# Attention and a 2-D FFT filter on one core: filter rows go from SBUF to SBUF, the last stage's pairs alternate, weight splits and flags stand apart

## The chip, the cores and the metric

The kernel runs on one core of a Trainium2 chip. A core has TensorE (PE in the profile; PEld is its loading of weights), VectorE (DVE), ScalarE (ACT), GpSimd (POOL) and SyncE (SP), and 16 DMA engines that serve the queues of SP, ACT and POOL. The metric is the time of one launch on the device in microseconds (us), as a median of several runs.

## The reference

The input x has 2048 rows of 1024 numbers in float32. Two layers follow one another, each an attention block and a spectral block, both behind a LayerNorm and both added to x:

```python
def _A_ref(x, wqkv, wo):
    qkv = (x @ wqkv).reshape(B, S, 3, H, Dh)          # H = 32 heads of 32
    ...
    scores = jnp.einsum("bhqd,bhkd->bhqk", q, k) * (Dh ** -0.5)
    p = _softmax(scores, axis=-1)
    o = jnp.einsum("bhqk,bhkd->bhqd", p, v)
    return o.transpose(0, 2, 1, 3).reshape(B, S, D) @ wo

def _B_ref(x, w_r, w_i):
    X = jnp.fft.rfft2(x, axes=(-2, -1))
    X = X * (w_r + 1j * w_i)
    return jnp.fft.irfft2(X, s=(S, D), axes=(-2, -1))

x = x + _A_ref(_layernorm(x), A_wqkv, A_wo)
x = x + _B_ref(_layernorm(x), B_w_r, B_w_i)
x = x + _A_ref(_layernorm(x), A_wqkv, A_wo)
x = x + _B_ref(_layernorm(x), B_w_r, B_w_i)
```

## The kernel before

`build` runs `attention` and then `spectral` for layer 0 and for layer 1. Much of the order is written out by hand: inside `tc.manual_schedule(engines=...)` the named engines take their instructions in the order of the code, and the other engines are ordered by the framework's scheduler. Behind both layers stands a general path that runs only if the flag `bad` is set; it isn't taken here.

**The spectral block.** The 2-D transform is done as products with constant matrices of sines and cosines. A first stage (`t1`, `fa`) turns the normalized input into 32 groups that stand in SBUF (`bh`). The middle is cut into 32 units (`UNITS`; 30 with four frequencies, the two at i = 14 and 15 with five), and a loop of 36 iterations runs over them as a pipeline. Iteration i does the forward transform along the rows for unit i (`fb`, products with `cb`, L1122, whose results ACT copies to B), splits the filtered unit i - 2 in two half-precision parts (`halves`, L1179 on ACT and L1180 on DVE), does the transform along the columns and the filter of unit i - 1 (`fc`: PE L1154, then DVE L1161 to L1164 and POOL L1168 and L1169), the first inverse step of unit i - 3 (`binv`, products with `cbi`, copied to U at L1115 by ACT) and the second of unit i - 4 (`cinv`, PE L1199 to L1202). `fc` ends with the load of the filter weights of the unit three further on (`loadw`, L1089), and in odd iterations 128 rows of the block's input y are loaded (L1235). The order of PE, ACT and SP in this loop is the order of the code.

What `cinv` leaves is a tile T of 128 partitions, four matrices j of 128 columns (256 KB). ACT copies it out of PSUM (L1204) into one of three buffers. The 128 partitions of a matrix are two halves r of 64 rows q. The next stage wants a matrix half as one partition of 64 x 128 numbers (32 KB): it sums over units, so units have to lie along the partitions. This turning of the layout goes by way of memory: SP stores T to `zt` in memory (L1205), and for every two units `turn` (L1209) reads 16 rows of 32 KB back into 16 partitions of `turned` (R or big in the rows of the trace, by layer). Which row lands on which partition is set by `row(i, r, j)` (L32), and the constant `mi` holds its rows in the same order.

**The last stage** of the block multiplies `turned` with `mi` (`ai`, L1252) in eight steps a, each in an even part (g = 0) and an odd part (g = 1, which is added to the even part in PSUM). `even(a)` needs only the rows of units 0 to 15; ACT scales its result (L1258) and POOL adds it to x (L1260). `odd(a)` needs the rows of units 16 to 31; DVE adds and subtracts its result (L1267). Four PSUM buffers hold the parts under way. The even parts 0 to 3 stand ahead of the first odd part, and behind odd(1) to odd(4) stands one more even part each. In layer 0 the splits of layer 1's first weights (`prep`) and statistics on DVE are done beside these steps, in layer 1 every step sends 1 MB of output (L1288).

**The flags.** `combine_flags` folds what was observed of the value ranges into the one flag `bad`: small operations on DVE, a transpose on PE, a reduction on DVE (L1426), a product of one number on PE (L1428), and two operations on DVE (L1430, L1431). In layer 1 it is run in three pieces, in the iterations 20, 21 and 22 of the loop.

Of the kernel before, what the change touches and what calls it, by code (L numbers as in the profile page):

```python
# [29 lines left out]


def row(i, r, j):  # L32
    return 8 * (8 * (i % 2) + 2 * j + r) + i % 16 // 2


def spec_consts():
# [303 lines left out]
PH0 = [("v", 0), ("k", 0), ("q", 0)]  # L340


def attention(nc, tc, layer, ap, xin, yd, wts, wo, cst, dram, flags):

# [295 lines left out]


    vk = [v_tiles(PH0[0], t) for t in range(8)]
    pre = [iter(()) if layer else prep(ph, m) for ph, m in zip(PH0, (lambda: load_x(1), None, lambda: load_x(4)))]

    def steps(g, n):
        for _ in range(n):
# [2 lines left out]
    with tc.manual_schedule(engines={mybir.EngineType.PE, mybir.EngineType.DVE, mybir.EngineType.Activation}):  # L651
        steps(pre[0], 1)
        for t in range(2, 4):
            load_x(t)
        for w in pre[1:]:
            steps(w, 1)
        for t in range(5, 10):
            load_x(t)
        save_x(range(8))
        m = [tile_root(nc, ap, cst, flags, layer, t) for t in range(4)]  # L660
        if layer == 0:
            for _ in range(2):
                next(m[0])
                steps(pre[0], 1)
        xn = norm_x(0, *flags.pop("rb"), 512)
        p = turn_x(xn)
        with tc.issue_after(flags["pin"].ins) if layer else nullcontext():
            next(m[1])
        steps(pre[0], 1)
        next(m[1])  # L670
        root = flags.pop("rb")
        run(pre[0])
        next(m[2])
        split_x(0, p, 4)
        xn = norm_x(1, *root)
        steps(vk[0], 8)
        next(m[2])
        root = flags.pop("rb")
        next(m[3])
        p = turn_x(xn)  # L680
        split_x(1, p, 8)
        next(m[3])
        xn = norm_x(2, *root)
        steps(vk[0], 12)
        p = turn_x(xn)
        split_x(2, p, 8)
        xn = norm_x(3, *flags.pop("rb"))
        high = flags["xn"]
        run(vk.pop(0))
        steps(vk[0], 8)  # L690
        p = turn_x(xn)
        split_x(3, p, 8)
        run(vk.pop(0))
# [307 lines left out]
    ps.close()  # L1001


def spectral(nc, tc, ap, yd, xout, a, cst, zt, fast, flags=None, nxt=None, join=None):

    ident = cst["ident"]
    psum, mid, work = Pools(tc, None), Pools(tc, "left"), Pools(tc, "left")
# [185 lines left out]
    def cinv(i):  # L1193
        g, k1, fs = UNITS[i]
        n = len(fs)
        U = Ut.pop(i)
        pt = ps.tile([128, 4, 128], F32, name="ps")
        for j in range(4 if n == 4 else 3):
            nc.tensor.matmul(pt[:, j], C["ci"][:, 8 * g + fs[j]], U[:, j], start=True, stop=True)  # L1199
        if n == 5:  # L1200
            for j in range(2):
                nc.tensor.matmul(pt[64 * j:64 * j + 64, 3], C["ci"][:, 8 * g + fs[3 + j], 0:64], U[:, 4 + j], start=True, stop=True)  # L1202
        t_ = p4.tile([128, 4, 128], F32, name="T")
        nc.scalar.copy(t_, pt)  # L1204
        nc.sync.dma_start(zt[i].rearrange("j p n -> p j n"), t_)  # L1205

    def turn(i):
        r0 = row(i, 0, 0)
        return nc.sync.dma_start(turned[r0:r0 + 121:8, UNITS[i][0]],  # L1209
                                 zt[i:i + 2].rearrange("i j (r q) n -> (i j r) q n", q=64))  # L1210

    for i in range(lead):
        loadw(i)
# [1 line left out]
    with tc.manual_schedule(engines=set(hold)) if fast else nullcontext():  # L1215
        for i in range(36):
            if i < 32:
                fb(i)
            if 0 <= i - 2 < 32 and fast:
                halves(i - 2)  # L1220
            if 0 <= i - 1 < 32:
                fc(i - 1)
            if 0 <= i - 3 < 32:
                binv(i - 3)
            if 0 <= i - 4 < 32:
                cinv(i - 4)
            if 7 <= i and i % 2:
                turn(i - 7)
            if i == 20 and join:
                joined = join(ps)  # L1230
            if 20 <= i < 23 and join:
                next(joined, None)
            if i % 2 and i < 32:
                t = i // 2
                nc.sync.dma_start(rest[:, t], yd[t * 128:(t + 1) * 128, :])  # L1235
        back = turn(30)
    psum.close()
    work.close()
    mid.close()
# [28 lines left out]
                if a == 7 and (t.start or op == ALU.subtract):  # L1268
                    next(m, None)

    with tc.manual_schedule(engines={mybir.EngineType.PE, mybir.EngineType.DVE}):
        for a in range(4):
            even(a)
        for a in range(8):
            odd(a)
            if 1 <= a < 5:
                even(a + 3)
            if nxt is not None:
                with tc.issue_after(back.ins) if a == 0 else nullcontext():
                    for _ in range(2):  # L1280
                        next(nxt, None)
                if 4 <= a < 4 + NST // 2:
                    for t in range(2 * a - 8, 2 * a - 6):
                        nc.vector.bn_stats(flags["st"][:, t, 0], ap.x[:, t, 0:512])
            else:
                sl = slice(a * 128, a * 128 + 128)
                if a < 7:
                    nc.sync.dma_start(xout[:, sl].rearrange("(t p) d -> p t d", p=128), ap.x[:, :, sl])  # L1288
                else:
                    for t, q in ((0, nc.sync), (8, nc.scalar)):  # L1290
                        q.dma_start(xout[t * 128:t * 128 + 1024, sl].rearrange("(t p) d -> p t d", p=128), ap.x[:, t:t + 8, sl])
# [112 lines left out]
def combine_flags(nc, ps, pool, flags, cst):  # L1404

    f = pool.tile([128, 6], F32, name="f4")
    fw, fb = (pool.tile([128, 1], F32, name=n) for n in ("fwm", "fwbm"))
    for m, n in ((fw, "w"), (fb, "wb")):
        nc.vector.reduce_max(m, flags[n], axis=AX.X)
    nc.vector.tensor_scalar(fw, fw, 1.0 / SW, None, op0=ALU.mult)  # L1410
    v = pool.tile([128, 1], F32, name="fv")
    nc.vector.tensor_reduce(v, flags["mv"][:, :, 1], axis=AX.X, op=ALU.min)
    nc.vector.tensor_scalar(f[:, 0:1], v, 1e-10, None, op0=ALU.is_ge)
    r = pool.tile([128, 1], F32, name="frm")
    nc.vector.reduce_max(r, flags["r"], axis=AX.X)
    nc.vector.tensor_scalar(f[:, 1:2], r, 1e20, None, op0=ALU.is_le)
    nc.vector.tensor_scalar(f[:, 2:3], fw, 1.0, None, op0=ALU.is_le)
    nc.vector.tensor_scalar(f[:, 3:4], fb, 2.0 ** -4, None, op0=ALU.is_le)
    nc.vector.tensor_scalar(f[:, 0:4], f[:, 0:4], -1.0, 1.0, op0=ALU.mult, op1=ALU.add)
    nc.vector.tensor_scalar(f[:, 4:5], fw, 2.0 ** -7, None, op0=ALU.is_ge)  # L1420
    nc.vector.tensor_scalar(f[:, 5:6], fb, 2.0 ** -12, None, op0=ALU.is_ge)
    yield
    t = ps.tile([128, 4, 128], F32, name="ps")
    nc.tensor.transpose(t[0:6, 0], f, cst["ident"])
    m = pool.tile([6, 1], F32, name="fa")
    nc.vector.reduce_max(m, t[0:6, 0], axis=AX.X)  # L1426
    yield
    nc.tensor.matmul(t[0:1, 1, 0:1], m, cst["sign"][0:6], start=True, stop=True)  # L1428
    b = pool.tile([1, 1], F32, name="fb")
    nc.vector.tensor_scalar(b, t[0:1, 1, 0:1], 2.0, 1.0, op0=ALU.add, op1=ALU.min)  # L1430
    nc.vector.tensor_copy(flags["bad"], b)  # L1431
# [6 lines left out]
def build(nc, tc, a):  # L1438
    with ExitStack() as ctx:
# [20 lines left out]
        }  # L1460
        nc.vector.memset(flags["r"], 0.0)
        x1 = dr.tile([2048, 1024], F32, name="x1")
        zt = dr.tile([32, 4, 128, 128], F32, name="zt")
        ap = AttnPools(tc)
        ap.open_small()
        x = a["x"]
        for o in (0, 512):
            nc.sync.dma_start(ap.x[:, 0, o:o + 512], x[0:128, o:o + 512])
        wts = [Weights(nc, ap, a["wp"], True, [flags["w"][:, i:i + 1] for i in range(32)], []),
               Weights(nc, ap, a["wp"], None, [], [])]  # L1470
        for layer in range(2):
            y = dr.tile([2048, 1024], F32, name=f"y{layer}")
            attention(nc, tc, layer, ap, x, y, wts[layer], a["wo"], cst, dr, flags)
            x = a["out"] if layer else x1
            if layer:
                spectral(nc, tc, ap, y, x, a, cst, zt, True, join=lambda ps: combine_flags(nc, ps, cp, flags, cst))
            else:
                spectral(nc, tc, ap, y, x, a, cst, zt, True, flags, (s for ph in PH0 for s in wts[1].prep(ph)))
        ap.close()
        bad = nc.values_load(flags["bad"][0:1, 0:1], min_val=0, max_val=1)  # L1480
        with tc.If(bad > 0):
            x = a["x"]
            for layer in range(2):
                y = dr.tile([2048, 1024], F32, name=f"gy{layer}")
                general_attention(nc, tc, x, y, a["wp"], a["wo"], cst)
                ap = AttnPools(tc)
                load_norm(nc, tc, cst, ap, y)
                x = a["out"] if layer else x1
                spectral(nc, tc, ap, y, x, a, cst, zt, False)
                ap.close()  # L1490


# [26 lines left out]
```

## Time and profile before

The launch takes 3677.62 us, the median of 3 runs (3676.18 to 3678.14). The page and the trace come from one profiled execution.

| | |
|---|---|
| Profiled execution | 3676.38 us, span 3674.6 us |
| Granted TensorE clock, mean over the span | 0.995 of full speed |
| Instructions | 80167 |
| Packets of all DMAs | 238284, 307.73 MB |
| HBM read / written | 165.65 MB / 135.20 MB |
| Stores of T (L1205) | 64, 256.0 KB each, 3.9 us from issue to landing |

The page begins with the busy time of each engine. Then it cuts the span into 40 slices of 91.9 us each. In the rows below, one digit is the busy share of a slice in tenths (9 is 90% or more), and DMA is the mean share of the 16 DMA engines:

```profile
PE   8999999999999999999899999999999999999997
...
ACT  5788888888888967768647888888888889677685
...
DMA  7122222232232442227651232323222324421378
```

The spectral blocks are the two places behind the first slice where the DMA row rises to 5 to 8 (slices 19 to 21, and 39 and 40): there the weights of the filter, y, T and the rows are moved. Between them the DMA share is 0.1 to 0.4.

### The profile page before, as it was taken

The numbers are of one execution on the slowest core, as the hardware profiler recorded it, in microseconds if no ns is written. First come the engines' busy times: TensorE is split into PE (matmuls) and PEld (weight loads), VectorE is DVE, ScalarE is ACT, GpSimd is POOL, SyncE is SP. The second block draws the span as 40 slices with busy tenths as digits, with TensorE's granted clock in tenths as the row PEclk, the third lists the DMA queues.
The fourth block names the chain that finished last, engine by engine and source line by source line (L and its number), as shares of the span: only waits on it lengthen the run. The fifth ranks groups of instructions, "written<-read, shape, count | busy, mean of one in ns | idle before, by whom it ended". The sixth has DMA issues, their size and how long they took to land. (4 is left out here: it accounts for less than half of the span.)

```text
span 3674.6 us, 80167 instructions
## 1 busy us (share of the span) xinstructions
PE 3600.5 (98%) x32663; PEld 1589.4 (43%) x32663; DVE 3104.2 (84%) x3726; ACT 2903.9 (79%) x3571; POOL 674.7 (18%) x802
## 2 busy tenths in 40 slices
PE   8999999999999999999899999999999999999997
PEld 5333433343344333378753334333433433333887
DVE  7799899989998988886568998999899989788754
ACT  5788888888888967768647888888888889677685
POOL 1022112211221110014510111111111111100144
PEclk9999999999999999999999999999999999999999
DMA  7122222232232442227651232323222324421378
GB/s 200 21 53 53 50 53 54 57 49 54 49 63 48 101 110 73 81 107 198 186 166 21 54 61 48 58 49 60 42 56 47 64 52 103 107 78 70 122 208 222
DMA packets 238284, 307.73 MB, mean 84 GB/s; under 512 B 77392, under 2 KB 156752, under 8 KB 236368
## 3 DMA queue, kind: packets, MB, share of 16 engines
q1 hardware_dynamic: 198944, 228.49, 20.6%
q0 software_dynamic: 37632, 73.43, 14.0%
q8 instruction: 258, 4.23, 0.5%
q14 instruction: 122, 1.00, 0.1%
q10 hardware_dynamic: 1328, 0.59, 0.1%
HBM read 165.65 MB, written 135.20 MB: 82 GB/s over the span
## 5 line engine op out<-in xcount | busy, mean ns | idle before, releaser
L740 ACT ACTIVATE p<-s,bias 128x1024 f32<-128x1024 f32 x2048 | 2170.8, 1112 | 457.6 <-PE s L736 439.3
L759 DVE TENSOR_TENSOR acc<-acc,p 128x1024 f32<-128x1024 f32 x896 | 1043.5, 1217 | 56.0 <-ACT p L740 55.0
L759 DVE TENSOR_TENSOR big<-big,p 128x1024 f32<-128x1024 f32 x448 | 522.2, 1218 | 38.5 <-ACT p L740 37.7
L759 DVE TENSOR_TENSOR R<-R,p 128x1024 f32<-128x1024 f32 x448 | 522.0, 1218 | 31.3 <-ACT p L740 30.1
L746 PE MATMUL o<-p,big 128*32 128x512 f32 x4096 | 492.5, 598 | 0.0
L746 PE MATMUL o<-p,R 128*32 128x512 f32 x4096 | 492.5, 598 | 0.0
L426 PEld LDWEIGHTS <-wqk 128*128 128x128 f16 x3072 | 275.6, 98 | 420.1 <-issue 127.3
L426 PE MATMUL x<-R,wqk 128*128 128x512 f16 x1440 | 338.1, 380 | 1.9 <-ACT big L488 1.2
L426 PE MATMUL x<-big,wqk 128*128 128x512 f16 x1440 | 338.2, 380 | 1.4 <-ACT R L488 0.7
L736 PEld LDWEIGHTS <-R 32*128 32x128 f16 x6144 | 114.8, 92 | 370.6 <-issue 312.8
L736 PEld LDWEIGHTS <-big 32*128 32x128 f16 x6144 | 114.2, 92 | 370.2 <-issue 312.0
L746 PEld LDWEIGHTS o<-p,big 128*32 128x32 f32 x4096 | 106.8, 109 | 261.7 <-issue 261.7
L746 PEld LDWEIGHTS o<-p,R 128*32 128x32 f32 x4096 | 106.8, 109 | 261.7 <-issue 261.7
L736 PE MATMUL s<-R 32*128 32x512 f16 x3072 | 213.7, 377 | 0.1
L736 PE MATMUL s<-Q,big 32*128 32x512 f16 x3072 | 212.7, 377 | 1.0 <-DVE mqk L460 1.0
L736 PE MATMUL s<-Q,R 32*128 32x512 f16 x3072 | 212.6, 378 | 1.0 <-DVE mqk L460 1.0
L736 PE MATMUL s<-big 32*128 32x512 f16 x3072 | 212.5, 377 | 0.1
L765 POOL DMA_DIRECT2D zd<-acc x112 | 92.4, 825 | 653.8 <-DVE z L775 304.0
L484 PE MATMUL x<-wv,big 128*128 128x256 f16 x1392 | 165.4, 275 | 3.0 <-DVE R L219 2.2
L484 PEld LDWEIGHTS <-big 128*128 128x128 f16 x1536 | 145.5, 98 | 48.9 <-issue 28.6
L484 PE MATMUL x<-wv,R 128*128 128x256 f16 x1392 | 165.4, 275 | 0.9 <-ACT R L392 0.9
L484 PEld LDWEIGHTS <-R 128*128 128x128 f16 x1536 | 145.5, 98 | 46.8 <-issue 26.1
(519 smaller groups left out, 4112.0 us busy)
## 6 DMA issues: line engine op xcount, KB each, us to landing
zd<-acc POOLq DMA_DIRECT2D x112, 256.0 KB, 4.2
wst<-in_wp SPq DMA_DIRECT2D x96, 256.0 KB, 3.3
zt<-T SPq DMA_DIRECT2D x64, 256.0 KB, 3.9
w<-in_w SPq DMA_DIRECT2D x60, 256.0 KB, 3.1
zd<-R POOLq DMA_DIRECT2D x56, 256.0 KB, 4.1
zt<-zr SPq DMA_DIRECT2D x224, 64.0 KB, 2.7
od<-ohl SPq DMA_DIRECT2D x56, 256.0 KB, 2.4
zd<-big POOLq DMA_DIRECT2D x56, 256.0 KB, 4.1
```

The lines of the kernel that those rows point to most:

```text
L426: nc.tensor.matmul(ps, a, b, start=i == 0, stop=i == 23)
L484: nc.tensor.matmul(ps[:, j], x[c][:, d, o:o + 128], w[:, n, d], start=i == 0, stop=i == 23)
L736: nc.tensor.matmul(s[h // 2][:, h % 2], K[g][r, a, kt * 128:kt * 128 + 128], Q[g][r, b, c * 512:c * 512 + 512], start=i == 0, stop=i == 2)
L740: nc.scalar.activation(p, s[hf], AF.Exp, bias=bias[g], scale=SCALE / (SQ * SQ))
L746: nc.tensor.matmul(O[g, c][32 * h:32 * h + 32], V[g][:, kt, 32 * h:32 * h + 32], P[g, c, kt, h // 2][:, h % 2], start=kt == 0, stop=kt == ...
L759: last_add = nc.vector.tensor_add(a, a, p)
L765: nc.gpsimd.dma_start(z, a[32 * j:32 * j + 32].rearrange("p a j n -> p (a j n)"), max_dma_last_dim=2048, **({"accum_op": ALU.add} if j els ...
```

## The change

Three edits are made.

**Rows.** `cinv` no longer stores T to memory. It issues four transfers, one for each matrix j, straight from T into two partitions of `turned`: r0 for the half r = 0, and r0 + 64 for r = 1. `zt` and `turn` are gone, and `row` is changed so that the two halves of a matrix lie 64 partitions apart; `mi` follows, since it is built with `row`.

**The last stage.** Two even parts stand ahead of odd(0), and behind each of odd(0) to odd(5) stands the even part two further on. ACT now also takes its instructions there in the order of the code. The splits of layer 1's weights are handed out by a table of steps, and those of the query chunk but the first step are passed on to `attention` as `rest`, which runs them ahead of its first query chunk.

**The flags.** `combine_flags` has more points at which it stops (`yield`), and is run in the iterations 12 to 23, one piece in each.

```diff
 def row(i, r, j):
-    return 8 * (8 * (i % 2) + 2 * j + r) + i % 16 // 2
+    return 64 * r + 16 * j + i % 16
...
-    pre = [iter(()) if layer else prep(ph, m) for ph, m in zip(PH0, (lambda: load_x(1), None, lambda: load_x(4)))]
+    pre = [iter(()), iter(()), rest] if layer else [prep(ph, m) for ph, m in zip(PH0, (lambda: load_x(1), None, lambda: load_x(4)))]
...
         t_ = p4.tile([128, 4, 128], F32, name="T")
         nc.scalar.copy(t_, pt)
-        nc.sync.dma_start(zt[i].rearrange("j p n -> p j n"), t_)
-
-    def turn(i):
-        r0 = row(i, 0, 0)
-        return nc.sync.dma_start(turned[r0:r0 + 121:8, UNITS[i][0]],
-                                 zt[i:i + 2].rearrange("i j (r q) n -> (i j r) q n", q=64))
+        for j in range(4):
+            r0 = row(i, 0, j)
+            back = nc.sync.dma_start(turned[r0:r0 + 65:64, g], t_[:, j])
+        return back
...
             if 0 <= i - 4 < 32:
-                cinv(i - 4)
-            if 7 <= i and i % 2:
-                turn(i - 7)
-            if i == 20 and join:
+                back = cinv(i - 4)
+            if i == 12 and join:
                 joined = join(ps)
-            if 20 <= i < 23 and join:
+            if 12 <= i < 24 and join:
                 next(joined, None)
...
-        back = turn(30)
...
-    with tc.manual_schedule(engines={mybir.EngineType.PE, mybir.EngineType.DVE}):
-        for a in range(4):
+    with tc.manual_schedule(engines={mybir.EngineType.PE, mybir.EngineType.DVE, mybir.EngineType.Activation}):
+        for a in range(2):
             even(a)
         for a in range(8):
             odd(a)
-            if 1 <= a < 5:
-                even(a + 3)
+            if a < 6:
+                even(a + 2)
             if nxt is not None:
                 with tc.issue_after(back.ins) if a == 0 else nullcontext():
-                    for _ in range(2):
+                    for _ in range((2, 1, 1, 1, 2, 1, 1, 0)[a]):
                         next(nxt, None)
...
-    for m, n in ((fw, "w"), (fb, "wb")):
-        nc.vector.reduce_max(m, flags[n], axis=AX.X)
+    nc.vector.reduce_max(fw, flags["w"], axis=AX.X)
+    yield
+    nc.vector.reduce_max(fb, flags["wb"], axis=AX.X)
+    yield
...
             else:
-                spectral(nc, tc, ap, y, x, a, cst, zt, True, flags, (s for ph in PH0 for s in wts[1].prep(ph)))
+                pre = [wts[1].prep(ph) for ph in PH0]
+                spectral(nc, tc, ap, y, x, a, cst, True, flags, chain(*pre[:2], islice(pre[2], 1)))
```

The order of the built instructions shows where this puts them. Below stands SP's queue in layer 0's loop, about the loads of the two units with five frequencies, before the change (line, operation, destination <- source with buffer numbers, shape; x4 is the same row four times):

```order
L1089 DMA w_20175<-in_w 128x640
L1205 DMA zt_85<-T_20205 128x4x128
L1089 DMA w_20242<-in_w 128x640
L1205 DMA zt_85<-T_20272 128x4x128
L1209 DMA R_93<-zt_85 16x8192
L1235 DMA big_89<-y0_133 128x1024
L1089 DMA w_20319<-in_w 128x512
L1205 DMA zt_85<-T_20345 128x4x128
L1089 DMA w_20400<-in_w 128x512
L1205 DMA zt_85<-T_20426 128x4x128
```

And the same place after it (the lines are those of the changed kernel, L1208 is the new transfer and L1232 the load of y):

```order
L1090 DMA w_20195<-in_w 128x640
L1208 DMA R_92<-T_20225 2x64x128 x4
L1090 DMA w_20265<-in_w 128x640
L1208 DMA R_92<-T_20295 2x64x128 x4
L1232 DMA big_88<-y0_132 128x1024
L1090 DMA w_20344<-in_w 128x512
L1208 DMA R_92<-T_20370 2x64x128 x4
L1090 DMA w_20428<-in_w 128x512
L1208 DMA R_92<-T_20454 2x64x128 x4
L1232 DMA big_88<-y0_132 128x1024
```

One store of T for each unit has become four transfers into R, and the return after every second unit is gone.

PE's rows at the beginning of layer 0's last stage before the change (the number in a name is the PSUM buffer's, its second appearance is the odd part):

```order
L1252 MATMUL ai_21658<-mi_66,R_93 128x128 x8
L1252 MATMUL ai_21670<-mi_66,R_93 128x128 x8
L1252 MATMUL ai_21682<-mi_66,R_93 128x128 x8
L1252 MATMUL ai_21694<-mi_66,R_93 128x128 x8
L1252 MATMUL ai_21658<-mi_66,R_93 128x128 x8
L1252 MATMUL ai_21670<-mi_66,R_93 128x128 x8
L1252 MATMUL ai_21737<-mi_66,R_93 128x128 x8
L1252 MATMUL ai_21682<-mi_66,R_93 128x128 x8
L1252 MATMUL ai_21763<-mi_66,R_93 128x128 x8
```

And after it:

```order
L1248 MATMUL ai_21737<-mi_66,R_92 128x128 x8
L1248 MATMUL ai_21749<-mi_66,R_92 128x128 x8
L1248 MATMUL ai_21737<-mi_66,R_92 128x128 x8
L1248 MATMUL ai_21771<-mi_66,R_92 128x128 x8
L1248 MATMUL ai_21749<-mi_66,R_92 128x128 x8
L1248 MATMUL ai_21804<-mi_66,R_92 128x128 x8
L1248 MATMUL ai_21771<-mi_66,R_92 128x128 x8
```

Before, the first odd part is the fifth row; now it is the third, and from there on one even part and one odd part alternate.

DVE's rows in layer 1's loop at the end of the flags before the change (`fa` is the reduction behind the transpose, `fb` and `fi` read the product of one number in the same PSUM tile; G, t_ and H belong to the units):

```order
L1164 TENSOR_TENSOR t__42405<-ps_42400,w_42195 128x256
L1180 TENSOR_TENSOR H_42333<-G_42332,H_42333 128x2x256
L1180 TENSOR_TENSOR H_42399<-G_42398,H_42399 128x2x256
L1426 TENSOR_REDUCE fa_42524<-ps_42522 6x1
L1430 TENSOR_SCALAR fb_42591<-ps_42522 1x1
L1431 CAST fi_82<-fb_42591 1x1
L1161 TENSOR_TENSOR G_42478<-ps_42480,w_42271 128x256
```

And after it:

```order
L1181 TENSOR_TENSOR H_42308<-G_42307,H_42308 128x2x256
L1428 TENSOR_REDUCE fa_42516<-ps_42514 6x1
L1181 TENSOR_TENSOR H_42388<-G_42387,H_42388 128x2x256
L1162 TENSOR_TENSOR G_42467<-ps_42469,w_42251 128x256
L1163 TENSOR_TENSOR t__42474<-ps_42469,w_42251 128x256
L1164 TENSOR_TENSOR G_42467<-ps_42469,w_42251 128x256
L1165 TENSOR_TENSOR t__42474<-ps_42469,w_42251 128x256
L1432 TENSOR_SCALAR fb_42586<-ps_42514 1x1
L1433 CAST fi_82<-fb_42586 1x1
```

The two last operations of the flags stood right behind the reduction; now five operations of the units stand between.

More of the change, by code (lines that the diff above doesn't have):

```diff
@@ L2 @@
 from contextlib import ExitStack, nullcontext
+from itertools import chain, islice
 import concourse.bass as bass
@@ L340, with attention @@
 PH0 = [("v", 0), ("k", 0), ("q", 0)]
-def attention(nc, tc, layer, ap, xin, yd, wts, wo, cst, dram, flags):
+def attention(nc, tc, layer, ap, xin, yd, wts, wo, cst, dram, flags, rest=()):
     W, prep = wts.W, wts.prep
@@ L654, in attention @@
             load_x(t)
-        for w in pre[1:]:
+        for w in pre[1:] if layer == 0 else ():
             steps(w, 1)
@@ L1001, in load_norm, with spectral @@
     ps.close()
-def spectral(nc, tc, ap, yd, xout, a, cst, zt, fast, flags=None, nxt=None, join=None):
+def spectral(nc, tc, ap, yd, xout, a, cst, fast, flags=None, nxt=None, join=None):
     ident = cst["ident"]
@@ L1412, in combine_flags @@
     nc.vector.tensor_reduce(v, flags["mv"][:, :, 1], axis=AX.X, op=ALU.min)
+    yield
     nc.vector.tensor_scalar(f[:, 0:1], v, 1e-10, None, op0=ALU.is_ge)
@@ L1415, in combine_flags @@
     nc.vector.reduce_max(r, flags["r"], axis=AX.X)
+    yield
     nc.vector.tensor_scalar(f[:, 1:2], r, 1e20, None, op0=ALU.is_le)
     nc.vector.tensor_scalar(f[:, 2:3], fw, 1.0, None, op0=ALU.is_le)
+    yield
     nc.vector.tensor_scalar(f[:, 3:4], fb, 2.0 ** -4, None, op0=ALU.is_le)
     nc.vector.tensor_scalar(f[:, 0:4], f[:, 0:4], -1.0, 1.0, op0=ALU.mult, op1=ALU.add)
+    yield
     nc.vector.tensor_scalar(f[:, 4:5], fw, 2.0 ** -7, None, op0=ALU.is_ge)
@@ L1462, in build @@
         x1 = dr.tile([2048, 1024], F32, name="x1")
-        zt = dr.tile([32, 4, 128, 128], F32, name="zt")
         ap = AttnPools(tc)
@@ L1470, in build @@
                Weights(nc, ap, a["wp"], None, [], [])]
+        pre = []
         for layer in range(2):
             y = dr.tile([2048, 1024], F32, name=f"y{layer}")
-            attention(nc, tc, layer, ap, x, y, wts[layer], a["wo"], cst, dr, flags)
+            attention(nc, tc, layer, ap, x, y, wts[layer], a["wo"], cst, dr, flags, *pre[2:])
             x = a["out"] if layer else x1
             if layer:
-                spectral(nc, tc, ap, y, x, a, cst, zt, True, join=lambda ps: combine_flags(nc, ps, cp, flags, cst))
+                spectral(nc, tc, ap, y, x, a, cst, True, join=lambda ps: combine_flags(nc, ps, cp, flags, cst))
             else:
-                spectral(nc, tc, ap, y, x, a, cst, zt, True, flags, (s for ph in PH0 for s in wts[1].prep(ph)))
+                pre = [wts[1].prep(ph) for ph in PH0]
+                spectral(nc, tc, ap, y, x, a, cst, True, flags, chain(*pre[:2], islice(pre[2], 1)))
         ap.close()
@@ L1488, in build @@
                 x = a["out"] if layer else x1
-                spectral(nc, tc, ap, y, x, a, cst, zt, False)
+                spectral(nc, tc, ap, y, x, a, cst, False)
                 ap.close()
```

## The prediction

> **What bounds the kernel now.** I read the page first, then the busy time by stretches, then the chain of waits, then the order in time on TensorE and on the DMA queues.
>
> The page's first part gives busy time, share of the span and instructions by engine:
>
> ```profile
> PE 3600.5 (98%) x32663; PEld 1589.4 (43%) x32663; DVE 3104.2 (84%) x3726; ACT 2903.9 (79%) x3571; POOL 674.7 (18%) x802
> ```
>
> TensorE (PE) is busy for 98% of the span. But the change touches only the spectral stages and their ends, so what counts is how things stand there. The busy time by stretches has for each start:end its length, then busy microseconds of PE, PEld, DVE, ACT and POOL, the granted clock, the DMA engines' mean busy share and GB/s:
>
> ```profile
> 1680.00:1720.00 40.00, 39.38 (x348) 35.30 (x346) 24.86 (x63) 34.41 (x90) 17.98 (x28) 1.00 0.77 212
> 3640.00:3675.00 35.00, 18.10 (x160) 17.94 (x160) 16.70 (x17) 4.10 (x4) 11.54 (x5) 0.80 0.89 244
> ```
>
> In the middle of a spectral loop PE works 39.38 of 40 us. The DMA engines are at 0.77, not far behind: a change of the DMA work can make them the bound. In the last 35 us they carry the end at 0.89, writing the output. The order in time on PE (start, length, matmuls, in brackets idle time before and who ended it) gives the pace of the loop and the first stop of layer 0's last stage:
>
> ```profile
> 1799.81 7.41 PE L1252 MATMUL ai<-mi,R 128*128 128x128 f32 x64 [0.72 <-ACT T L1204]
> 1809.48 3.81 PE L1252 MATMUL ai<-mi,R 128*128 128x128 f32 x32 [2.26 <-DMA wst<-in_wp]
> ...
> 3583.75 1.47 PE L1122 MATMUL ps<-cb,R 128*128 128x256 f16 x12
> ...
> 3588.16 1.47 PE L1122 MATMUL ps<-cb,R 128*128 128x256 f16 x12
> ```
>
> From one unit's first product to the next one's pass 4.41 us (3588.16 - 3583.75). At 1799.81 four even parts run, 1.85 us each (7.41 / 4); then PE has nothing until the filter rows of the last units are in SBUF, and the odd parts start at 1809.48. The releaser named is another DMA, but an odd part reads only the rows and the constant mi, so I take it to be the last row transfer. The chain that ended last shows the same place in layer 1:
>
> ```profile
> 3626.55 3.99 DMA zt<-T
> ...
> 3630.59 4.98 DMA big<-zt
> ...
> 3635.91 2.04 PE ai L1252 x16
> ```
>
> T goes to memory in 3.99 us and comes back in 4.98 us, and the odd parts start at 3635.91.
>
> **What the transfers cost now.** The queue's own rows (start, time of the issue) show where a layer's row traffic begins, and what an issue like the new one takes:
>
> ```profile
> 1660.65 0.38 SPq L1205 DMA_DIRECT2D zt<-T  x1
> ...
> 3489.40 0.38 SPq L1205 DMA_DIRECT2D zt<-T  x1
> ...
> 3590.49 0.48 SPq L1209 DMA_DIRECT2D big<-zt  x1
> ```
>
> So the row traffic now spans 148.8 us in layer 0 (1660.65 to 1809.48) and 146.5 us in layer 1 (3489.40 to 3635.91), with all of it hidden but the last stop.
>
> The DMA view of one stretch counts packets by size and gives the share of the 16 engines' time that they took. From 1662 to 1666 almost only T is being moved, in pieces of 512 bytes:
>
> ```profile
> DMA packets 559, 0.31 MB, mean 77 GB/s; under 512 B 31, under 2 KB 535, under 8 KB 559
> q1 hardware_dynamic: 559, 0.31, 25.6%
> ```
>
> From 3400 to 3410 one 512 KB store goes in 4 KB pieces:
>
> ```profile
> DMA packets 144, 0.52 MB, mean 52 GB/s; under 512 B 16, under 2 KB 16, under 8 KB 144
> q1 hardware_dynamic: 144, 0.52, 12.8%
> ```
>
> From 3631 to 3636 one return of rows goes from zt to 16 partitions:
>
> ```profile
> DMA packets 48, 0.52 MB, mean 105 GB/s; under 512 B 32, under 2 KB 32, under 8 KB 32
> q1 hardware_dynamic: 48, 0.52, 48.1%
> ```
>
> The second: 12.8% of 160 us are 20.5 us for 128 pieces, 160 ns for 4 KB. The first: 25.6% of 64 us are 16.4 us; 24 pieces of 2 KB at half of 160 ns are 1.9 us, which leaves 14.5 us for 504 pieces, **28.7 ns for 512 bytes**. The third is the one that matters most: 16 data packets (48 less 32 small ones) for a transfer with 16 destination rows. One packet is one row of 32 KB, 2.4 us each (48.1% of 80 us by 16), and 38.5 us of packets fit in 5 us, so they run side by side. **This transfer was cut by its destination rows.**
>
> **The change part by part.**
>
> *Rows from SBUF to SBUF.* Per unit the change takes away one store of T (256 KB) and half a return (512 KB), and issues four transfers of 64 KB. Each has 128 source rows and two destination rows, r0 and r0 + 64, and each destination row is filled by 64 pieces of 512 bytes, since a source partition holds only 128 numbers of it. That is 512 pieces for a unit, where T's store alone had 512 before. If the work is cut by destination rows as in the row above, two engines carry each transfer and the other fourteen nothing. If these are the same two each time, each has 4 x 64 = 256 pieces a unit: 256 x 28.7 ns = 7.35 us, against the 4.41 us that PE needs for a unit. The two engines keep up only below 12.5 ns a piece (4.41 less some 1.2 us of other loads, by 256).
>
> The loads that those two engines share with the rest are these, in the stretch 1660 to 1806:
>
> ```profile
> big<-y SPq DMA_DIRECT2D x14, 512.0 KB, 7.0
> w<-in_w SPq DMA_DIRECT2D x24, 256.0 KB, 3.6
> ...
> w<-in_w SPq DMA_DIRECT2D x2, 320.0 KB, 4.8
> ```
>
> One of 16 engines carries of a y load 8 pieces of 4 KB (1.28 us) and of a w load 8 of 2 KB (0.64 us; 0.80 for the large ones). The sum on one of the two engines, for one layer: rows 32 x 256 x 28.7 ns = 235.1 us, y 14 x 1.28 = 17.9 us, w 24 x 0.64 + 2 x 0.80 = 17.0 us, together **270.0 us**. They start with the first T as before, and the odd parts start when the last row is in: 270.0 - 148.8 = +121.2 us in layer 0 and 270.0 - 146.5 = +123.5 us in layer 1, **+244.7 us** in all.
>
> The wait that this adds: T has three buffers, so ACT's copy into T (L1204) waits for the rows of three units before. Behind it in ACT's order stand the next unit's copies of B and U (L1115), for which PE waits; PE then runs at the transfers' pace. On SP the next w load and y load stand behind four issues, 4 x 0.48 = 1.9 us instead of some 0.6, inside 4.41 us: nothing, unless the queue fills, and then the two engines are the limit anyway. POOL's queue has no part in it.
>
> No row shows a piece that goes from SBUF to SBUF. Bounds by the nearest rows: at the rate of the 4 KB pieces 160 / 8 = 20.0 ns; at that of the 32 KB packets into a single partition 2.4 us / 64 = 37.6 ns. I take 28.7 ns, of the row that already reads T in the same pieces. The ends give 163.8 + 34.9 = 198.7 us and 308.0 + 34.9 = 342.9 us a layer, so +102.1 us and +390.5 us in all.
>
> [...]
>
> *Pairs alternate.* Only two even parts stand ahead of odd(0), and the other two now come behind it: 2 x 1.85 = 3.7 us of PE that used to lie in the stop. I cost it at nothing: in layer 1 the output's DMA (0.89 in the last stretch) covers it, in layer 0 DVE's adds and statistics. Without that cover it is 3.7 us a layer. PE will come to this stage from half idleness; at the clock of 0.80 in the row above, its 26 us here would take some 6 us more. I leave that to the range.
>
> *Weight splits and flags apart.* Two weight splits of layer 1 move into the attention, before the query chunk that needs them: nothing. The flags' last step now stands a unit behind the reduction that feeds it. Before, DVE waited there for PE:
>
> ```profile
> 3570.55 0.15 DVE L1430 TENSOR_SCALAR fb<-ps 1x1 f32<-1x1 f32 x1 [4.24 <-PE ps L1428]
> ```
>
> and PE's unit took 8.84 us instead of 4.41:
>
> ```profile
> 3570.44 1.48 PE L1122 MATMUL ps<-cb,R 128*128 128x256 f16 x12
> ...
> 3579.28 1.54 PE L1122 MATMUL ps<-cb,R 128*128 128x256 f16 x12
> ```
>
> That is worth 4.4 us where PE sets the pace. Under the rows' traffic it is worth nothing.
>
> **The rivals.** *The transfers spread (faster).* If the pieces are shared out by the source's 128 rows, or successive transfers take turns on other pairs, no engine has more to do than before, and the tail shortens. The last T is copied at 3626.55; three further issues (1.44 us) and a landing like T's (3.9 us by the page) put odd(0) at 3631.9, 4.0 us earlier; in layer 0, from a copy that ends at 1799.8, at 1805.1, 4.4 us earlier. With the flags' 4.4 us: 3676.4 - 12.8 = **3663.6 us**. For it: the engines now share T's store, which has 128 rows on both sides. Against it: the only transfer here with few destination rows had just one packet for each. It decides at the count of engines: four would still carry 128 x 28.7 ns = 3.7 us of rows and 1.1 us of loads a unit, eight 1.8 and 1.1 us, below 4.41.
>
> [...]
>
> *Each piece pays twice (slower still).* If reading from SBUF and writing to it do not overlap on an engine, a piece takes 57.4 ns: 470.2 + 34.9 = 505.1 us a layer, +714.9 us, **4391 us**. For it: nothing but that no such piece has been seen. Against it: T's pieces, read from SBUF and written to memory, already do both in 28.7 ns.
>
> **How the numbers follow.** The profiled execution took 3676.4 us, 1.2 us below the median of the runs. Two engines: 3676.4 + 244.7 = **3921 us**, chance 0.80. Spread: 3664 us, chance 0.15. Pieces twice: 4391 us, chance 0.05. The range is that of the first case, 3676.4 + 102.1 = 3778 to 3676.4 + 390.5 = 4067, and leaves out the other 0.20. What a measurement of this kernel can tell from no change is about 0.2%, 7 us: the spread case clears it unless half its gain is lost, so faster 0.13, same 0.02, slower 0.85.
>
> **What would show it.** Right: PE's period in the spectral loops near 8.6 us instead of 4.41, ACT's T copy waiting for a DMA, the DMA share in the loops falling to about 0.15 to 0.2 while nothing else is busy, and the gap from the first row transfer to the first odd part near 270 us. Wrong: the period stays at 4.41 us and the new transfers land within some 4 us of issue; then the engines share them. If the period is between, the price of a piece is what I missed.

## The result, and the profile after

The changed kernel takes **3913.9 us**, the median of 4 runs (3913.35 to 3914.88), against 3677.88 us before: a ratio of 1.0642, 95% interval 1.0624 to 1.0661, 236.0 us longer. The forecast was 3921 us, the range 3778 to 4067. The profiled execution took 3914.88 us, with a span of 3913.1 us, 238.5 us longer than the span before.

The page, first the busy time, then two rows of the 40 slices (97.8 us each):

```profile
PE 3680.7 (94%) x32663; PEld 1629.1 (42%) x32663; DVE 3114.3 (80%) x3726; ACT 2898.2 (74%) x3571; POOL 670.6 (17%) x802
...
PE   8999999999999999976589999999999999999874
...
DMA  6132223322234422333251232223222344212334
```

PE runs no more products than before (32663), though they count as 80 us more of busy time, at a mean granted clock of 0.973 against 0.995. It is now less busy in slices 18 to 20 and at the end, and in the same slices the DMA share, which used to rise to 7 and 8, stays at 2 to 4. Both wait, and the busy time by stretches shows it for the loop of layer 0:

```profile
1680.00:1720.00 40.00, 28.91 (x201) 22.94 (x201) 14.11 (x33) 19.74 (x50) 9.52 (x13) 0.89 0.32 83
```

In the same stretch before, PE was busy for 39.38 us and the DMA share was 0.77. The order in time names the wait. First ACT, then SP's queue, between two units of that loop (a line of SP's queue gives the start and the time of its issues; x4 is four of them):

```profile
1706.64 0.59 ACT L1205 COPY T<-ps 128x512 f32<-128x512 f32 x1 [5.01 <-DMA R<-T]
...
1715.28 0.58 ACT L1205 COPY T<-ps 128x512 f32<-128x512 f32 x1 [4.46 <-DMA R<-T]
```

```profile
1702.78 5.97 SPq L1208 DMA_DIRECT2D R<-T  x4
1708.85 1.58 SPq L1232 DMA_DIRECT2D big<-y  x1
1710.54 0.37 SPq L1090 DMA_DIRECT2D w<-in_w  x1
1711.00 7.68 SPq L1208 DMA_DIRECT2D R<-T  x4
```

From one copy of T to the next pass 8.64 us instead of 4.41, and ACT stands for some 5 us of them until a buffer of T comes free. SP too is held: four issues take 5.97 and 7.68 us, where an issue took 0.48 us before. With rows alone under way, the DMA view of a stretch at layer 0's end reads:

```profile
DMA packets 1509, 0.76 MB, mean 38 GB/s; under 512 B 23, under 2 KB 1509, under 8 KB 1509
...
q1 hardware_dynamic: 1509, 0.76, 14.2%
```

That is 1915 to 1935 us: many transfers are queued, and they take no more than 14.2% of 16 engines, 2.3 engines' worth (two engines that are always busy are 12.5%; with two, the spans of packets overlap a little). If transfers took turns on other engines, a full queue would show more of them. The 1486 pieces here (1509 less 23 small packets) are those of 11.6 transfers, so each transfer has two small packets; the experiments come back to that. Shared by two engines, 1486 pieces in 20 us are one piece in 26.9 ns on each. In layer 1, from 3855 to 3868 us, it is one in 23.6 ns:

```profile
DMA packets 1118, 0.56 MB, mean 43 GB/s; under 512 B 18, under 2 KB 1118, under 8 KB 1118
```

The rows' time in a layer runs from the first issue of L1208 to the odd parts (behind the stop in the last stage):

```profile
L1208 SPq DMA_DIRECT2D R<-T x128: 505/1620/4566, 1661.2 to 1933.0; - x128
L1208 SPq DMA_DIRECT2D big<-T x128: 506/1374/4451, 3627.6 to 3864.9; - x128
```

```profile
1911.71 5.90 PE L1248 MATMUL ai<-mi,R 128*128 128x128 f32 x32 [4.28 <-ACT T L1205]
1941.11 27.95 PE L1248 MATMUL ai<-mi,R 128*128 128x128 f32 x224 [23.50 <-DMA R<-T]
...
3842.90 4.55 PE L1248 MATMUL ai<-mi,big 128*128 128x128 f32 x32
3871.48 27.07 PE L1248 MATMUL ai<-mi,big 128*128 128x128 f32 x224 [24.04 <-DMA big<-T]
```

1941.11 - 1661.2 = 279.9 us in layer 0 and 3871.48 - 3627.6 = 243.9 us in layer 1, against 148.8 and 146.5 us before: +131.1 and +97.4, **+228.5 us** of the 238.5. The other 10 us lie outside: 6.6 us from layer 0's odd parts to layer 1's first transfer (1686.5 us against 1679.9), 2.9 us from layer 1's odd parts to the end (41.6 against 38.7), and 0.5 us ahead of the first transfer.

### The profile page after: what moved, and what is told of

Its sections match the earlier page's. It is cut to its first block, busy times and chain, and to the rows that moved or that the text cites. A ratio compares the mean times of both kernels' runs of the same rounds, so it can differ in the third digit from the quotient of the medians.

```text
span 3913.1 us, 80433 instructions
## 1 busy us (share of the span) xinstructions
PE 3680.7 (94%) x32663; PEld 1629.1 (42%) x32663; DVE 3114.3 (80%) x3726; ACT 2898.2 (74%) x3571; POOL 670.6 (17%) x802
## 5 line engine op out<-in xcount | busy, mean ns | idle before, releaser
L1205 ACT COPY T<-ps 128x512 f32<-128x512 f32 x64 | 37.4, 585 | 235.5 <-DMA R<-T 123.1
L1181 DVE TENSOR_TENSOR H<-G,H 128x512 f16<-128x512 f32 (+1 forms) x68 | 55.4, 819 | 162.2 <-ACT H L1180 162.0
L1155 PE MATMUL ps<-cc,B 128*128 128x128 f32 x520 | 93.7, 313 | 90.7 <-ACT B L1116 90.2
```

The lines of the kernel that those rows point to most:

```text
L1155: nc.tensor.matmul(pc[:, j].rearrange("p r f -> p (r f)"), B[:, POS[n][o + j]], C["cc"][:, 8 * g + fs[o + j]], start=True, stop=True)
L1181: nc.vector.tensor_sub(lo, gs, hi)
```

## The experiments

**The rows' part undone** (the run norows). In the changed kernel, T goes to memory and comes back as before:

```diff
-    return 64 * r + 16 * j + i % 16
+    return 8 * (8 * (i % 2) + 2 * j + r) + i % 16 // 2
...
-        for j in range(4):
-            r0 = row(i, 0, j)
-            back = nc.sync.dma_start(turned[r0:r0 + 65:64, g], t_[:, j])
+        nc.sync.dma_start(zt[i].rearrange("j p n -> p j n"), t_)
...
+            if 7 <= i and i % 2:
+                back = turn(i - 7)
```

> The changed kernel with the rows sent through memory again (store of T, return of 16 rows, the old row order); pairs, weight splits and flags stay as changed. Theory (the rows alone made the time longer, since two DMA engines carry them): the loop is back at 4.41 us a unit, the flags' step of 4.4 us is gone, and the even parts behind odd(0) cost 0 to 3.7 us a layer: 3677.9 - 4.4 = 3673.5 us, up to 3681 us. Rival (the other two edits have a share in the 236 us): clearly over 3690 us.

3682.92 us, median of 11 runs; ratio to before 1.0017 (1.0008 to 1.0026). The large loss is gone, so it takes the rows' part to make it. What is left is 0.17% slower than before, not faster: a little over the bound of 3681. The flags' gain did not come, since in this kernel the scheduler put their last operations right behind one another again, and DVE waited for PE as before:

```profile
3565.12 0.14 DVE L1437 TENSOR_SCALAR fb<-ps 1x1 f32<-1x1 f32 x1 [4.24 <-PE ps L1435]
```

**The rows' part alone** (rowsonly), put into the kernel before (the diff above, reversed).

> The kernel before with the rows alone changed (four transfers from T to two partitions each); the last stage, the splits and the flags as before. Theory (two engines carry the rows): as long as the changed kernel, 3914 us, less at most the 3.7 us a layer of even parts that lie in the stop here, so 3906 to 3920 us. Rival (the edits lengthen the time only together): well under 3900 us.

3909.35 us, ratio 1.0634 (1.0618 to 1.0651). The rows make the loss by themselves, but for some 4 us. The rows' time is that of the changed kernel, 279.6 us in layer 0 (1659.3 to 1938.89) and 244.4 in layer 1 (3621.3 to 3865.71).

**Two buffers for T** (tbufs2) in place of three.

```diff
-    pw, p4 = work("sp_pw", lead), work("sp_p4", 3)
+    pw, p4 = work("sp_pw", lead), work("sp_p4", 2)
```

> The changed kernel with two buffers for T in place of three. Theory (the two engines are always busy with rows): with two buffers one unit's rows are still under way while the next T is copied, so the time stays at 3914 us, at most 20 us more. Rival (each unit waits for the latency of its transfers, and three buffers set how many are in flight): the period goes from about 8 to about 12 us a unit, some 250 us more, about 4160 us.

3908.09 us (one run), and the rows' time is 280.4 and 241.9 us, about as with three buffers. Fewer buffers cost nothing: the wait is for something that is always busy, not for a latency that more buffers would hide.

**The suspected cost doubled** (double): each transfer is issued twice.

```diff
-        for j in range(4):
-            r0 = row(i, 0, j)
-            back = nc.sync.dma_start(turned[r0:r0 + 65:64, g], t_[:, j])
+        for j in range(8):
+            r0 = row(i, 0, j % 4)
+            back = nc.sync.dma_start(turned[r0:r0 + 65:64, g], t_[:, j % 4])
```

> The changed kernel with each of the four transfers issued twice (the same data to the same place): the suspected cost doubled. Theory (two engines carry all pieces one after the other): 2 x 32 x 256 more pieces on each engine at 23 to 28.7 ns are 377 to 470 us more, 4290 to 4385 us. Rival (the wait is the latency of a unit's transfers, or SP's issues): four more issues of 0.5 us a unit, at most 2 x 32 x 2 us = 130 us more, under 4050 us.

4330.43 us (one run), 416.5 us more than the changed kernel and inside what the engines' load gave. The first issue of each layer, and the first odd parts:

```profile
L1208 SPq DMA_DIRECT2D R<-T x256: 510/1602/4484, 1662.1 to 2157.3; - x128
L1208 SPq DMA_DIRECT2D big<-T x256: 506/1387/4542, 3852.3 to 4281.9; - x128
```

```profile
2165.49 9.78 PE L1248 MATMUL ai<-mi,R 128*128 128x128 f32 x59 [50.78 <-DMA R<-T]
...
4288.31 11.96 PE L1248 MATMUL ai<-mi,big 128*128 128x128 f32 x92 [53.44 <-issue]
```

The rows' time is now 503.4 and 436.0 us, 223.5 and 192.1 us more than with single transfers. The 32 x 256 = 8192 added pieces on an engine thus cost **27.3 ns each in layer 0 and 23.5 ns in layer 1**. That is the pace at which the rows ran alone in the changed kernel, 26.9 and 23.6 ns. What does not double is 279.9 - 223.5 = 56.4 us and 243.9 - 192.1 = 51.8 us.

**Half of the transfers from ACT's queue** (actq).

```diff
-            back = nc.sync.dma_start(turned[r0:r0 + 65:64, g], t_[:, j])
+            back = (nc.sync if j < 2 else nc.scalar).dma_start(turned[r0:r0 + 65:64, g], t_[:, j])
```

> The changed kernel with two of a unit's four transfers issued by ACT in place of SP. [...] Rival (each queue has two engines of its own): half the load on each, 128 pieces and the loads, 4.3 to 4.8 us a unit, and ACT pays its issues: 3690 to 3730 us.

Against that rival, the same engines on both queues had been put at 3895 to 3930 us. 3894.43 us (one run) is half a microsecond below these bounds: 20 us less than the changed kernel, where other engines for the second queue would have given 200 less. From 1915 to 1921 us, with rows alone under way from both queues (q1 is SP's, q10 is ACT's), the DMA view reads:

```profile
q1 hardware_dynamic: 226, 0.11, 7.7%
q10 hardware_dynamic: 226, 0.11, 7.5%
```

Together they take 15.2% of 16 engines, where one queue took 14.2%. Two queues get no more than one, so both are served by the same engines. Of the 20 us, 14.7 lie in the rows' time (274.1 and 235.0 us); what shortened it was not tried.

**One destination row for each transfer** (onerow): eight of 32 KB, the same pieces and the same layout.

```diff
         for j in range(4):
-            r0 = row(i, 0, j)
-            back = nc.sync.dma_start(turned[r0:r0 + 65:64, g], t_[:, j])
+            for r in range(2):
+                r0 = row(i, r, j)
+                back = nc.sync.dma_start(turned[r0:r0 + 1, g], t_[64 * r:64 * r + 64, j])
```

> The changed kernel with each transfer cut in two: eight transfers of 32 KB a unit, each from 64 partitions into one partition, the same 512 pieces of 512 bytes a unit and the same row order. Theory as the prediction put it (a transfer is cut by its destination rows): one row means one engine, 512 pieces on it at 23 to 28 ns are 12 to 14 us a unit, about 8 x 32 x 2 us = 500 us over the kernel before, about 4200 us. [...] Rival (SBUF to SBUF is slow however it is shared): still about 3914 us. [...]

3796.25 us, ratio 1.0328 (1.0313 to 1.0342): half of the loss is gone. That rules out the theory in its plain form (one row, one engine) and the rival (as slow however it is shared). A third time had been put down for the case that many engines share such a transfer and SP's issues, at 0.5 us each, set the pace: 4.4 to 4.7 us a unit, 3664 to 3682 us. It is not that either, and SP's queue in the loop shows one reason:

```profile
1701.34 5.79 SPq L1209 DMA_DIRECT2D R<-T  x8
1707.40 0.35 SPq L1090 DMA_DIRECT2D w<-in_w  x1
1707.85 5.76 SPq L1209 DMA_DIRECT2D R<-T  x8
1713.71 0.53 SPq L1233 DMA_DIRECT2D big<-y  x1
1714.35 0.36 SPq L1090 DMA_DIRECT2D w<-in_w  x1
1714.81 6.09 SPq L1209 DMA_DIRECT2D R<-T  x8
```

SP issues almost without a gap, eight transfers in 5.8 us (0.72 us each, where I had put 0.5), 6.4 us a unit with the loads (256 issues in the 202.7 us from 1661.9 to 1864.6). The transfers themselves land 3.7 us after their issue in the median, 2.6 us at best:

```profile
DMA to landing us min/median/max: 2.6/3.7/8.8
```

Sixty-four pieces on one engine would need 64 x 23.5 = 1.5 us for one transfer and 12 us for a unit, longer than the 6.4 us in which a unit passes here, so more than one engine carries these transfers. How many is seen in the small packets, from 1660 to 1860 us:

```profile
DMA packets 25927, 23.23 MB, mean 116 GB/s; under 512 B 4661, under 2 KB 20661, under 8 KB 25907
```

In this stretch SP issues 251 transfers of rows and 40 loads. If each load has 16 small packets, 4661 - 640 = 4021 are left, 16 for each transfer of one row. With two rows there were two. In the kernel before, the stores of T, the returns and the loads also come out at about 16 (1394 small packets for 88 transfers, from 1660 to 1806 us). My estimate from these counts is that 16 engines carry a transfer with one row and two a transfer with two: it takes each small packet for one engine, as the two small packets and the 14.2% of the full queue go together with two rows, and was not tested by itself. A further rival, that a partition of the destination can't take its pieces faster, falls too: in this run, from 1709.78 to 1710.05 us, 62 of the 64 pieces of one transfer start on their way into one partition, 4.4 ns a piece.

**Half of these issues from POOL** (onerowpool).

```diff
-                back = nc.sync.dma_start(turned[r0:r0 + 1, g], t_[64 * r:64 * r + 64, j])
+                back = (nc.gpsimd if r else nc.sync).dma_start(turned[r0:r0 + 1, g], t_[64 * r:64 * r + 64, j])
```

> onerow with the four transfers of the half r = 1 issued by POOL in place of SP. In onerow SP issues one after the other (eight in 5.8 us) and a unit takes about 6.5 us. Theory (onerow is bound by SP's issues, not by engines): SP needs 4 x 0.72 + 0.36 + 0.27 = 3.5 us a unit, POOL its 2 us of work and 4 x 0.8 us (its stores of zd), 5.2 us, so 1.2 us a unit less: 3796 - 77 = 3720 us, 3695 to 3745. Rival (32 KB transfers are slow on the engines): 3780 us or more.

3770.92 us (one run): 25 us less, a third of what was expected, and by neither theory. SP now has gaps, so it no longer sets the pace alone, but POOL's issues stand among its own work, and in one unit ACT waits for that:

```profile
1712.35 0.62 ACT L1180 CAST H<-G 128x512 f16<-128x512 f32 x1 [4.44 <-POOL G L1170]
```

What bounds this kernel was not followed further.

**The two large buffers in SBUF exchanged** (swap), since the rows' time was 36 us longer in layer 0 than in layer 1 for the same transfers:

```diff
-        self.lay(self.low("at_x", 1).tile([128, 16384], F32, name="big"),
-                 self.right("at_r", 1).tile([128, 16384], F32, name="R"))
+        self.lay(self.right("at_r", 1).tile([128, 16384], F32, name="big"),
+                 self.low("at_x", 1).tile([128, 16384], F32, name="R"))
```

> The changed kernel with the two large SBUF buffers exchanged: what lay in the one (the rows' destination in layer 0) now lies in the other. In the changed kernel a layer's rows took 279.9 us in layer 0 and 243.9 us in layer 1, from the first issue to the first odd part. Theory (the place of the destination in SBUF sets a piece's price): the two times change places, about 244 us in layer 0 and 280 us in layer 1. Rival (something else of the layer does it: what is loaded beside the rows, or the order): they stay where they are, 280 and 244 us. The total stays within 10 us of 3914 us by both.

3914.89 us (one run). The first issues and the odd parts of its two layers:

```profile
L1208 SPq DMA_DIRECT2D R<-T x128: 505/1374/4447, 1660.9 to 1897.5; - x128
L1208 SPq DMA_DIRECT2D big<-T x128: 506/1622/4898, 3591.4 to 3865.1; - x128
```

```profile
1904.51 7.75 PE L1248 MATMUL ai<-mi,R 128*128 128x128 f32 x47 [20.21 <-DMA wst<-in_wp]
...
3872.61 9.64 PE L1248 MATMUL ai<-mi,big 128*128 128x128 f32 x58 [28.75 <-DMA big<-T]
```

243.6 us in layer 0 and 281.2 us in layer 1: they have changed places. Which of the two large buffers the rows go to sets the price, and not the loads of y beside them, which go to the other buffer: with rows alone under way it is one piece in 23.6 ns in layer 0 (1270 pieces from 1880 to 1895 us) and in 27.0 ns in layer 1 (1482 from 3845 to 3865).

**The even parts** (evens4): norows with four even parts ahead of odd(0), and ACT not bound to the order of the code:

```diff
-    with tc.manual_schedule(engines={mybir.EngineType.PE, mybir.EngineType.DVE, mybir.EngineType.Activation}):
-        for a in range(2):
+    with tc.manual_schedule(engines={mybir.EngineType.PE, mybir.EngineType.DVE}):
+        for a in range(4):
...
-            if a < 6:
-                even(a + 2)
+            if 1 <= a < 5:
+                even(a + 3)
```

> The kernel norows with the last stage in the order of before (four even parts ahead of odd(0), ACT not in the order of the code there); its splits and flags stay as changed. Theory (in norows the even parts moved behind odd(0) cost 3.2 us in layer 0 and 1.9 us in layer 1, read from its trace against that of before): 5 us less than norows, so within 0.1% of the kernel before, about 3677 us. Rival (the splits handed out in other steps, or the moved flags, cost it): as long as norows, 3683 us.

3677.96 us, median of 11; ratio to before 1.0003 (0.9993 to 1.0012), against 1.0017 (1.0008 to 1.0026) with the pairs alternating. By the ratios the difference is the 5 us that were expected, but the intervals overlap, and the profiled executions of the two (3681.91 and 3680.84 us) are only 1.1 us apart. The price of this edit is thus suggested and not shown. The run undoes two things at once, the order of the parts and that of ACT.

**The flags, two tries** (flagsonly and flags2), both on the kernel before. First other iterations for the three pieces:

```diff
-            if i == 20 and join:
+            if i == 18 and join:
                 joined = join(ps)
-            if 20 <= i < 23 and join:
+            if i in (18, 20, 22) and join:
                 next(joined, None)
```

> The kernel before with the flags' three pieces run in the iterations 18, 20 and 22 in place of 20, 21 and 22, so that the two last operations on DVE stand a unit behind the reduction. (In norows the scheduler had put them right behind the reduction again, and the unit of 8.8 us was there as before.) Theory: the wait of 4.2 us on DVE and PE's long unit go, 4.4 us less, a ratio of 0.9988. Rival (a PSUM buffer held for two iterations more stops PE elsewhere): no change, 1.0000, or slower.

3679.82 us, ratio 1.0007 (0.9998 to 1.0016): no gain, as the rival had it, but not by its mechanism. DVE stops at each of the flags' operations:

```profile
3561.71 0.28 DVE L1426 TENSOR_REDUCE fa<-ps 6x1 f32<-6x128 f32 x1 [4.70 <-PE ps L1424]
3561.92 0.40 DVE L1161 TENSOR_TENSOR G<-ps,w 128x256 f32<-128x256 f32 x1
...
3573.54 0.15 DVE L1430 TENSOR_SCALAR fb<-ps 1x1 f32<-1x1 f32 x1 [3.07 <-PE ps L1428]
3573.72 0.14 DVE L1431 CAST fi<-fb 1x1 int32<-1x1 f32 x1
3573.79 0.40 DVE L1161 TENSOR_TENSOR G<-ps,w 128x256 f32<-128x256 f32 x1
```

The products of a unit (L1161) come right behind and are late each time. So the second try leaves the iterations at 20, 21 and 22, ties the flags' second and third piece behind a unit's products, and changes nothing else:

```diff
-                fc(i - 1)
+                last = fc(i - 1)
...
-                next(joined, None)
+                with tc.issue_after(last.ins) if i > 20 else nullcontext():
+                    next(joined, None)
```

> The kernel before with the flags' second and third piece tied on DVE behind the products of the unit in whose iteration they stand (L1161 to L1164), as the changed kernel has its last piece; PE's order is as before. In flagsonly the two waits of DVE for PE (4.7 and 3.1 us) stood ahead of a unit's products, and the units took 7.3 and 8.3 us. Theory (DVE's place decides, not the distance between the flags' operations): no product waits behind a flag, PE keeps its 4.41 us a unit, 4 us less than before, a ratio of 0.9988 to 0.999. Rival (the lost time isn't on the path that sets the end of the loop): 1.0000.

3673.95 us, median of 11; ratio 0.9989 (0.9980 to 0.9998). PE's first products of the units around the flags, in order of time:

```profile
3568.23 1.47 PE L1122 MATMUL ps<-cb,R 128*128 128x256 f16 x12
...
3572.85 1.48 PE L1122 MATMUL ps<-cb,R 128*128 128x256 f16 x12
...
3577.27 1.47 PE L1122 MATMUL ps<-cb,R 128*128 128x256 f16 x12
```

4.62 and 4.42 us: the unit of 8.84 us is gone. This is the one version that is faster than the kernel before, by 0.1%, with the upper end of its interval just below 1.

**The last two units alone from SBUF to SBUF** (tail), on top of flagsonly, with one row a transfer:

```diff
-        nc.sync.dma_start(zt[i].rearrange("j p n -> p j n"), t_)
+        if i < 30:
+            nc.sync.dma_start(zt[i].rearrange("j p n -> p j n"), t_)
+            return
+        for j in range(4):
+            for r in range(2):
+                r0 = row(i, r, j)
+                back = (nc.scalar if r and i == 31 else nc.sync).dma_start(turned[r0:r0 + 1, g], t_[64 * r:64 * r + 64, j])
```

> flagsonly with the rows of the last two units alone (30 and 31) sent from SBUF to SBUF, in eight transfers of one destination row each, those of unit 31 half from SP and half from ACT; the other thirty units go through memory. Theory (16 engines share such a transfer, and what it costs is the issue, some 0.7 us): unit 31's rows are issued within 3 us and land 3.7 us later, about 3 us a layer earlier than by memory: 6 us less than flagsonly, a ratio to before of 0.997. Rival (unit 30's eight issues stand ahead on SP, and the landing takes as long as store and return): no gain on flagsonly.

3694.68 us, ratio 1.0049 (1.0035 to 1.0062): slower than before. In SP's queue the return of units 28 and 29 now stands behind twelve issues:

```profile
1797.75 0.55 SPq L1216 DMA_DIRECT2D R<-zt  x1
1800.17 10.71 SPq L1211 DMA_DIRECT2D R<-T  x12
1810.93 0.59 SPq L1216 DMA_DIRECT2D R<-zt  x1
```

With 4.98 us, as such a return took before, it lands at 1815.9, and the odd parts of layer 0 started at 1816.74 instead of 1809.48. Counted from the first even part, the odd parts start 5.8 us later than before in layer 0 and 4.8 us later in layer 1; where the rest of the 17 us lies was not followed. The edit put the return there; whether a tail with the return ahead would gain was not tried.

## Why the prediction was right

*Two engines carry the rows: right.* The runs norows and rowsonly give the whole loss to this edit, tbufs2 and double show a load and not a latency, actq shows that the engines are the same from another queue, and the full queue at 14.2% of 16 engines, with two small packets for each transfer, shows their number. The word that the prediction gave to the cause was too narrow: it said that a transfer is cut by its destination rows. onerow, with one row a transfer, is not confined to one engine: it leaves 16 small packets for the 64 pieces of a transfer, where two rows leave two, and a unit passes in 6.4 us where one engine would need 12. What decides how many engines share a transfer was not shown beyond these two cases.

*The sum: right by terms that missed on both sides.* It said 270.0 us a layer: 235.1 for the pieces and 34.9 for the other loads.

| us | predicted | layer 0 | layer 1 |
|---|---|---|---|
| price of a piece, ns | 28.7 | 27.3 | 23.5 |
| 8192 pieces on one engine | 235.1 | 223.5 | 192.1 |
| all else in the rows' time | 34.9 | 56.4 | 51.8 |
| rows' time | 270.0 | 279.9 | 243.9 |
| more than before | 121.2 / 123.5 | 131.1 | 97.4 |

The price came from T's pieces on their way to memory and was too high, by 1.4 and 5.2 ns. A part of that can be read from the views: the prediction divided the time of packets by their number, and on a busy engine packets overlap. In the changed kernel, the 14.2% from 1915 to 1935 us are 45.4 us of packets, some 30 ns a piece, while a piece passed every 26.9 ns. Against that, the rest was mis-sized: beside the pieces 16.9 and 21.5 us a layer more pass than the packets of w and y take by themselves. The runs don't divide it. That the total came within 7 us of the forecast is in part luck, since the errors went against each other: the rows' time was 9.9 us longer than forecast in layer 0 and 26.1 us shorter in layer 1, and 10 us lie outside it.

*The rest of the sum: not at nothing.* 10 us lie outside the rows' time, and the sum had none there. In rowsonly, whose span is 232.6 us longer than before, 3.9 us lie outside it, so some 6 come with the other two edits, within a scatter of a few us (in kernels with the same code up to there, layer 0's first transfer starts anywhere from 1658.7 to 1662.1 us). norows and evens4 suggest some 5 us for the last stage's edit, which the prediction cost at nothing, or at 7.4 us if nothing covered it. Their traces show less of it: from the first even part to PE's next stage in layer 0, and to the end in layer 1, pass 44.1 and 51.0 us in norows and 43.3 and 50.2 in evens4, so 0.8 us a layer. So whether the cover that the prediction named (DVE in layer 0, the output in layer 1) holds in full stays open. The clock that it left to the range cost little: the 224 products from odd(0) on took 27.95 and 27.07 us, where norows took 26.88 and 26.87.

*The flags: right in size.* What they are worth under the rows' traffic was not measured by itself. Where PE sets the pace, flags2 shows 0.11% (4 us; 0.7 to 7.4 by the interval), against 4.4 us predicted. But what frees them is DVE's place behind the unit's products, not the distance that the change is named for: flagsonly stood them two iterations apart and gained nothing.

*The rivals.* Spread over the engines (3664 us): not with two rows. onerow shows that the pieces can be spread, and that SP then issues almost all the time; but half of the issues on POOL gave back only 25 us, so what bounds it then is not shown. Each piece twice (4391 us): at 23.5 to 27.3 ns a piece, no.

*What would show it.* The period was to be near 8.6 us; it is 8.9 us in layer 0 (1688.60 to 1911.07 for 25 units, by ACT's copies of T) and 7.8 us in layer 1 (3652.13 to 3846.12), where a piece is cheaper. The DMA share was to fall to 0.15 to 0.2: it is 0.14 where rows run alone, and 0.32 in the loop, where the loads come in bursts.

## What to carry to other kernels

A transfer's bytes and pieces don't say how long it takes (the same 512 pieces a unit took 8.9 us in layer 0 with two rows a transfer, and 6.4 us with one); ask first how many engines will share it (here the DMA share of a full queue, 14.2% of 16 engines, told it), then multiply the pieces on one engine by their price and hold that against the period of the loop that it serves. Cutting it so that more engines share it is paid in issues (eight of 0.72 us a unit in onerow, 5.8 of its 6.4 us), and the issuing queue may be the next bound: count those against the same period. A small operation on an engine whose order is fixed costs what stands behind it while it waits (in flagsonly DVE waited 4.70 and 3.07 us at the flags, with a unit's products behind), so give it a place behind the work that others wait for.

## What was not expected of the hardware

The same transfers from SBUF to SBUF cost 27.3 ns a piece into one of the two large buffers and 23.5 ns into the other, 16% more, and the difference followed the buffer when the two were exchanged (279.9 and 243.9 us became 243.6 and 281.2). Why one buffer is dearer was not found. And an issue of such a transfer on SP took 0.5 us at least, and 1.4 to 1.6 us in the median where the two engines' queues were full; eight in a row to one partition each, in onerow, took 0.72 us each.
